# Chunk A loads of the next batch go ahead of waiting chunk C loads in the load list of a Fourier-mixing and SwiGLU kernel

## The chip, the cores and the metric

One NeuronCore of a Trainium2 chip. The time is the device time of one execution in microseconds (us), as the median of several runs. A traced execution gives the profile; its clock starts at the first instruction of the program.

## The reference

The input x has 8 batches of 3008 rows of 256 values. Each batch goes through a two-dimensional Fourier transform, of which the real part is kept; its rows then go through a gated feed-forward block.

```python
X = np.fft.fft(np.fft.fft(x, axis=1), axis=2).real   # x: (8, 3008, 256)
x = X.reshape(8 * 3008, 256)
g = x @ w_gate                                       # w_gate, w_val: (256, 1536)
out = (g / (1 + np.exp(-g)) * (x @ w_val)) @ w_out   # w_out: (1536, 256)
```

Inputs and output are float32; the matrix products inside the kernel run in bfloat16.

## The kernel before, in words

**Two kinds of work share the engines.** The transform uses the symmetries of a real input: rows that mirror each other are added and subtracted ("folded"), on POOL for all batches but the first, and the folded rows are multiplied by tables of sines and cosines on PE. What results are two tiles per 512 columns, Pt and Qt, from which the rows of the output at a frequency k and at M - k follow as a sum and a difference (the letters p and m, "plus" and "minus", in the names below). The feed-forward block works through 24 such tiles of columns, each in 12 units (one unit for each 128 of the 1536 hidden columns), 288 units in all. The program is written out unit by unit in this order, and each engine executes its own instructions strictly in the order in which they are written (a manual schedule).

**One unit.** PE makes the gate g and the value v from Pt and Qt (`part_a`, L737), adds the correction for the minus half one unit later (`part_b`, L774), and between these multiplies earlier hidden tiles by w_out (`OWork`, L697). ACT applies the gate function (L749, L764, L778, L782). The product of gate and value is taken by DVE (L765, L783), or, in six of twelve units of a tile from tile 3 on ("split" units), by POOL (L757 for hp, L779 for hm), with DVE preparing the plus and minus values first: es (L752) and two vv (L754, L756). The vv tiles have four buffers, so a third split unit's first vv waits for POOL's product of the first split unit. Accumulators lie in PSUM: three banks named g, three named v, two named o. The finished o is copied to an output buffer ev by ACT (L703, L706; four buffers, one for 256 rows), and written to memory by SP (L709, two or three DMAs for one buffer).

**The loads.** Each batch is loaded in two chunks: chunk A into XA (20 DMAs: 16 small at L129, 4 large at L131), chunk C into XC (39 DMAs at L140, L143, L145). XA holds one batch; XC has two halves, for two batches. All these loads and all output writes are issued by SP, in the order of the program. A load may be issued when the fold that read the old contents is past its last read (L165). Eight semaphores are used in turn for SP's DMAs, so that one DMA is issued only when the one eight before it has landed.

**The load list.** Loads are not written into the program at once, but put into a list, `loads`. At the head of each unit `run_loads` writes the first three of it (if the first is of chunk A) or the first six. When a fold has taken its last read of XA or XC, two units later `load_next` puts the next loads at the end of the list: after a chunk A fold those of A for the next batch; after a chunk C fold those of C for the next two batches (78 DMAs, marked with the number of the first of them). When a fold begins whose loads still wait, `fold_step` writes out all of the list up to the last of these loads ("rush").

**Folds on POOL.** A fold of one half of a chunk is seven steps: two with SDf (L165), which read XA or XC, and then EOf, Af, CE and BB (L168 to L184) from SDf. The steps are spread over the units (`spread`) and stand in POOL's order among the products L757 and L779. The fold of C(2) and C(3), batches 2 and 3, is spread over units 25 to 44, that of A(2) over 45 to 63, that of A(3) from 65 on.

**At the place of the change.** At unit 11 the 78 loads of C(2) and C(3) are put into the list; they follow the loads of A(1). At unit 22 the loads of A(2) are put at its end: 36 loads of C(3) are then still waiting. At units 23, 24 and 25 six loads each are written, and at unit 25 the fold of C(2) begins and rushes the last 18. A(2) follows at three a unit. Later batches' A loads are put into a list that is empty.

Of the kernel before, what the change touches and what calls it, by code (L numbers as in the profile page):

```python
# [31 lines left out]
def kernel(  # L32
# [8 lines left out]
    nc = tc.nc  # L41
# [76 lines left out]
    def up_block(b, j, n):  # L118
        return rows_at(b, 2 * j - 1, [[2 * D, n], [R * D, 4], [1, 2 * D]])

    def down_set(b, a, j, L, n):

        return rows_at(b, R * (a + 1) - 2 * j, [[2 * L * D, n], [-2 * D, L], [1, 2 * D]])
# [3 lines left out]
    def load_a(b, q):  # L127
        X3 = XA.rearrange("p a q d -> p a (q d)")
        return ([lambda h=h: q.dma_start(out=X3[LA * h:LA * (h + 1), 0:4, :],  # L129
                                         in_=up_block(b, JA - LA * h, LA)) for h in range(NA)] +  # L130
                [lambda a=a: q.dma_start(out=X3[:, 4 + a, :], in_=down_set(b, a, JA, LA, NA)) for a in range(4)])  # L131

    def load_c(b, q):
        bb = b % 2
        steps = []
        for qq in range(2):
            p0 = 64 * qq
            for h in range(NC_):
                up = rows_at(b, 2 * (JC - LC * h) - 1 + qq, [[2 * D, LC], [R * D, 4], [1, D]])
                steps.append(lambda p=p0 + LC * h, up=up: q.dma_start(out=XC[p:p + LC, 0:4, bb, :], in_=up))  # L140
            for a in range(4):
                down = rows_at(b, R * (a + 1) - 2 * JC + 1 - qq, [[2 * LC * D, NC_], [-2 * D, LC], [1, D]])
                steps.append(lambda p=p0, a=a, down=down: q.dma_start(out=XC[p:p + NCR, 4 + a, bb, :], in_=down))  # L143
        pm = 64 + NCR
        steps.append(lambda: q.dma_start(out=XC[pm:pm + 1, 0:4, bb], in_=rows_at(b, 0, [[R * D, 1], [R * D, 4], [1, D]])))  # L145
        return steps
# [681 lines left out]
    def load_next(what):  # L828
        kind, b = what
        if kind == "A":  # L830
            if b + 1 < B:
                loads.extend((("A", b + 1), fn) for fn in load_a(b + 1, nc.sync))
        else:
            b = b // 2 * 2 + 2
            if b < B:
                loads.extend((("C", b), fn) for fn in load_c(b, nc.sync) + load_c(b + 1, nc.sync))
# [34 lines left out]
    loads = []  # L871
# [3 lines left out]
    for i, u in enumerate(units):  # L875
# [25 lines left out]
        for what in act_at.pop(i, ()):  # L901
            load_next(what)
# [38 lines left out]
```

## Time and profile before

| | before |
|---|---|
| median of 3 runs | 690.73 us (689.88 to 691.08) |
| the profiled execution | 688.43 us |
| its span, first to last instruction | 686.7 us |
| PE busy | 662.1 us (96%) |
| POOL busy | 570.3 us (83%) |
| DVE busy | 513.5 us (75%) |
| ACT busy | 432.4 us (63%) |
| granted TensorE clock over the span | 0.995 |
| read from memory, written to it | 29.39 MB, 24.65 MB |

PE is the matrix engine, DVE the vector engine, ACT the scalar engine, POOL the general-purpose engine; SP only issues DMAs. The page's second part cuts the span into 40 slices of 17.2 us and gives the busy share of each engine in tenths; "PEclk" is the clock that the matrix engine was granted. The chain of work that ended last is followed back from the last instruction. A timeline row gives start, duration, engine, source line, operation, "written <- read" tiles, shapes and count; a bracket at its end gives how long the engine was idle before and what ended that. SPq is SP's issuing sequencer. Rows of windows give the stretch, its length, busy time and count of PE, PE's weight loads, DVE, ACT and POOL, then the granted clock, the busy share of the DMA engines and GB/s. Where the profile names a DMA as the releaser of a wait, the name can be that of a neighbour on the same semaphore.

### The profile page before, as it was taken

What the parts mean: (1) busy time and instruction counts of PE and PEld (TensorE: products, weight loads), DVE (VectorE), ACT (ScalarE), POOL (GpSimd) and SP (SyncE); (2) the same over time, 40 slices, a digit from 0 to 9 for tenths busy, and PEclk for the clock granted to TensorE, in tenths of its full rate; (3) what the DMA queues carried; (4) which work ended last, traced back from release to release, by engine and by line L of the source; (5) the groups of instructions that cost most, each with busy time, mean ns of one, the idle gap of its engine ahead of it and who ended that gap; (6) DMA issues with size and microseconds to landing.
All of it is one profiled execution on the core that took longest, in us unless ns stands there. A gap on an engine that the chain in (4) does not pass through costs nothing.

```text
span 686.7 us, 13388 instructions
## 1 busy us (share of the span) xinstructions
PE 662.1 (96%) x4374; PEld 414.7 (60%) x4374; DVE 513.5 (75%) x919; ACT 432.4 (63%) x764; POOL 570.3 (83%) x558
## 2 busy tenths in 40 slices
PE   7989999999799999999999999999999999999997
PEld 5446665665455666565665666656666666656676
DVE  8886668786567877777777787777777787788862
ACT  7676655665456666565666666666666666666663
POOL 9991977999499999999998998998999655668920
PEclk9999999999989999999999999999999999999999
DMA  9555225323512412235125111117111011111112
GB/s 229 105 87 109 74 59 156 110 67 107 165 31 66 121 47 68 72 95 160 36 62 145 38 44 35 48 40 155 36 48 48 32 41 38 46 32 47 47 47 70
DMA packets 49767, 52.56 MB, mean 77 GB/s; under 512 B 7130, under 2 KB 41026, under 8 KB 49698
## 3 DMA queue, kind: packets, MB, share of 16 engines
q1 hardware_dynamic: 46514, 49.35, 26.4%
q0 software_dynamic: 3184, 2.36, 2.4%
q8 instruction: 34, 0.56, 0.4%
q14 instruction: 35, 0.29, 0.1%
HBM read 29.39 MB, written 24.65 MB: 79 GB/s over the span
## 4 chain that ended last, share of the span: by engine, by line
PE 80%; DVE 8%; POOL 4%; issue 4%; ACT 1%; DMA 1%; SPq 0%; DVEq 0%; ACTq 0%; POOLq 0%
PE o L697 31%; PE v L737 16%; PE g L737 15%; PE g L774 8%; PE v L774 4%; PE v L572 3%; DVE vv L756 2%; DVE Pt L604 1%; PE g L572 1%; POOL hm L779 1%; DVE es L752 1%; DMA out_dram<-ev 1%; DVE vv L754 1%; POOL SDf L165 1%; PE g L880 1%
## 5 line engine op out<-in xcount | busy, mean ns | idle before, releaser
L757 POOL TENSOR_TENSOR hp<-sgv,vv 128x512 bf16<-128x512 f32 (+1 forms) x126 | 160.3, 1274 | 39.9 <-DVE vv L754 26.8
L697 PE MATMUL o<-Wo,hm 128*128 128x256 bf16 (+2 forms) x1140 | 170.5, 274 | 0.0
L697 PE MATMUL o<-Wo,hp 128*128 128x256 bf16 (+2 forms) x1140 | 169.6, 273 | 0.0
L779 POOL TENSOR_TENSOR hm<-sgv,vv 128x512 bf16<-128x512 f32 (+1 forms) x126 | 159.8, 1273 | 9.9 <-ACT sgv L778 8.2
L697 PEld LDWEIGHTS <-hp 128*128 128x128 bf16 (+2 forms) x1140 | 112.0, 98 | 68.2 <-issue 7.8
L697 PEld LDWEIGHTS <-hm 128*128 128x128 bf16 (+2 forms) x1140 | 112.4, 99 | 65.8 <-issue 6.4
L752 DVE SCALAR_TENSOR_TENSOR es<-bc,w,v 128x512 f32<-128x512 f32 (+1 forms) x126 | 93.7, 744 | 52.4 <-PE v L737 52.3
L765 DVE TENSOR_TENSOR hp<-sg,v 128x512 bf16<-128x512 f32 (+2 forms) x162 | 107.8, 665 | 33.0 <-ACT sg L764 32.1
L783 DVE TENSOR_TENSOR hm<-sg,v 128x512 bf16<-128x512 f32 (+2 forms) x162 | 107.4, 663 | 24.2 <-ACT sg L782 15.3
L782 ACT ACTIVATE sg<-g 128x512 f32<-128x512 f32 (+2 forms) x162 | 94.7, 585 | 46.8 <-PE g L774 46.0
L764 ACT ACTIVATE sg<-g 128x512 f32<-128x512 f32 (+2 forms) x162 | 94.5, 583 | 38.2 <-PE g L737 35.6
L737 PE MATMUL v<-Pt,Wp 128*128 128x512 bf16 (+2 forms) x288 | 108.4, 376 | 6.3 <-DVE vv L756 6.2
L737 PE MATMUL g<-Pt,Wp 128*128 128x512 bf16 (+2 forms) x288 | 108.5, 377 | 1.5 <-ACT sgv L778 1.1
L778 ACT ACTIVATE sgv<-g 128x512 f32<-128x512 f32 (+1 forms) x126 | 75.4, 598 | 53.7 <-PE g L774 39.8
L737 PE MATMUL g<-Qt,Wq 128*128 128x512 bf16 (+2 forms) x288 | 108.2, 376 | 0.5 <-DVE Qt L604 0.5
L774 PE MATMUL g<-Qt,Wm 128*128 128x512 bf16 (+2 forms) x288 | 108.1, 375 | 0.0
L754 DVE SCALAR_TENSOR_TENSOR vv<-v,es 128x512 f32<-128x512 f32 (+1 forms) x126 | 87.0, 690 | 18.6 <-POOL hp L757 1.0
L756 DVE SCALAR_TENSOR_TENSOR vv<-v,es 128x512 f32<-128x512 f32 (+1 forms) x126 | 85.7, 680 | 12.9 <-POOL hm L779 12.8
L749 ACT ACTIVATE sgv<-g 128x512 f32<-128x512 f32 (+1 forms) x126 | 75.1, 596 | 30.6 <-PE g L737 23.0
L165 POOL TENSOR_TENSOR SDf<-XA 128x1024 f32<-128x1024 f32 x28 | 66.0, 2363 | 24.8 <-DMA XC<-in_x_dram 14.7
L737 PEld LDWEIGHTS <-Wp 128*128 128x128 bf16 x576 | 56.4, 98 | 45.3 <-issue 7.7
L703 ACT COPY ev<-o 128x512 f32<-128x512 f32 x90 | 52.7, 586 | 34.3 <-PE o L697 29.1
(170 smaller groups left out, 731.0 us busy)
## 6 DMA issues: line engine op xcount, KB each, us to landing
out_dram<-ev SPq DMA_DIRECT2D x96, 128.0 KB
XA<-in_x_dram SPq DMA_DIRECT2D x32, 256.0 KB
XA<-in_x_dram SPq DMA_DIRECT2D x112, 64.0 KB
XC<-in_x_dram SPq DMA_DIRECT2D x210, 16.0 KB
XC<-in_x_dram SPq DMA_DIRECT2D x56, 60.0 KB
out_dram<-ev SPq DMA_DIRECT2D x12, 120.0 KB
out_dram<-ev SPq DMA_DIRECT2D x10, 112.0 KB
XA<-in_x_dram SPq DMA_DIRECT2D x1, 1024.0 KB
```

Of the source, the lines that this page charges most:

```text
L697: nc.tensor.matmul(ps[:n, j, :], hts[minus][:, f, c:c + n], Wo[:, f, :], start=(f == 0), stop=(f == nF - 1))
L737: nc.tensor.matmul(ps[:, :w], Wt[:, gv, fs], src[:, :w], start=start, stop=stop, skip_group_check=True)
L752: stt(es[:, :w], bc[t][:, :w], w0[:, f:f + 1], e[:, :w], op0=Alu.mult, op1=Alu.add)
L754: stt(vp[:, :w], o[:, :w], -0.5, es[:, :w], op0=Alu.mult, op1=Alu.add)
L756: stt(vm[:, w - 1::-1], o[:, :w], 0.5, es[:, :w], op0=Alu.mult, op1=Alu.add)
L757: nc.gpsimd.tensor_tensor(hts[t][0][:, f, :w], sg[:, :w], vp[:, :w], op=Alu.mult)
L764: nc.scalar.activation(sg[:, :w], g[:, :w], AF.Silu)
L765: nc.vector.tensor_tensor(hts[t][0][:, f, :w], sg[:, :w], v[:, :w], op=Alu.mult)
L774: nc.tensor.matmul(ps[:, :w], Wm[:, gv, f * P:(f + 1) * P], Qt[:, :w], start=False, stop=True, skip_group_check=True)
L779: nc.gpsimd.tensor_tensor(hts[t][1][:, f, :w], sg[:, :w], v[:, :w], op=Alu.mult)
L782: nc.scalar.activation(sg[:, :w], g[:, :w], AF.Silu)
L783: nc.vector.tensor_tensor(hts[t][1][:, f, w - 1::-1], sg[:, :w], v[:, :w], op=Alu.mult)
```

## The change

`load_next` puts the loads of the next batch's chunk A not at the end of the list but ahead of the first waiting chunk C load, where there is one.

```diff
@@ load_next @@
         kind, b = what
         if kind == "A":
             if b + 1 < B:
-                loads.extend((("A", b + 1), fn) for fn in load_a(b + 1, nc.sync))
+                at = next((k for k, (w_, _) in enumerate(loads) if w_[0] == "C"), len(loads))
+                loads[at:at] = [(("A", b + 1), fn) for fn in load_a(b + 1, nc.sync)]
         else:
             b = b // 2 * 2 + 2
             if b < B:
```

Written out, the program differs on SP alone, and in one stretch: after the third load of C(3) come the 20 loads of A(2), with one group of three outputs after the sixth, and then the other 36 loads of C(3). At units 23 to 25 three A loads each are written, and at unit 25 the fold of C(2) rushes 11 loads of A and, because all 78 loads carry the mark of C(2), 36 of C(3). The outputs that stood between the loads of A(2) now follow the last load of C(3). The orders of PE, DVE, ACT and POOL are unchanged.

```
before                                     after
C(3): 15 loads                             C(3): 3 loads
outputs x3                                 A(2): 6 loads
C(3): 24 loads                             outputs x3
A(2): 6 loads                              A(2): 14 loads
outputs x3                                 C(3): 36 loads
A(2): 9 loads                              outputs x12
outputs x3
A(2): 5 loads
outputs x6
C(4) ...                                   C(4) ...
```

## The prediction

> **What bounds the kernel now.** I read the page first (totals, the row of slices, the chain), then each engine's timeline where the change can act, then busy time by windows there.
>
> ```profile
> span 686.7 us, 13388 instructions
> PE 662.1 (96%) x4374; PEld 414.7 (60%) x4374; DVE 513.5 (75%) x919; ACT 432.4 (63%) x764; POOL 570.3 (83%) x558
> ...
> POOL 9991977999499999999998998998999655668920
> ...
> PE 80%; DVE 8%; POOL 4%; issue 4%; ACT 1%; DMA 1%; SPq 0%; DVEq 0%; ACTq 0%; POOLq 0%
> ```
>
> PE is busy 96% of the span and holds 80% of the chain, so a microsecond that PE loses is lost unless it would have been lost anyway. POOL is full through most slices too, except the sixth (86 to 103 us) and the eleventh (172 to 189 us). Those two dips decide this case. Of the six times that a batch queues the next chunk A, only one finds chunk C loads waiting, the one at unit 22: 36 loads of C(3) wait, and A(2) now goes ahead of them. So the change acts once, near 86 us. From the C(4) loads on, SP's list is the same as before.
>
> ```profile
> 77.04 4.67 POOL L165 TENSOR_TENSOR SDf<-XA 128x1024 f32<-128x1024 f32 x2
> ...
> 106.83 2.36 POOL L165 TENSOR_TENSOR SDf<-XC 128x1024 f32<-128x1024 f32 x1 [7.90 <-DMA XA<-in_x_dram]
> ...
> 112.63 1.22 POOL L779 TENSOR_TENSOR hm<-sgv,vv 128x480 bf16<-128x480 f32 x1
> ...
> 156.58 2.37 POOL L165 TENSOR_TENSOR SDf<-XA 128x1024 f32<-128x1024 f32 x1
> ...
> 174.66 1.27 POOL L757 TENSOR_TENSOR hp<-sgv,vv 128x512 bf16<-128x512 f32 x1
> 185.94 2.34 POOL L165 TENSOR_TENSOR SDf<-XA 128x1024 f32<-128x1024 f32 x1 [10.00 <-DMA out_dram<-ev]
> ...
> 229.60 1.27 POOL L757 TENSOR_TENSOR hp<-sgv,vv 128x512 bf16<-128x512 f32 x1 [0.39 <-DVE vv L754]
> ```
>
> In POOL's timeline (start, duration, instruction, idle before in brackets) POOL stands idle for 7.90 us until 106.83, where the fold of C(3) begins: its loads are the ones that SP has just issued (below). From there POOL runs without a gap to 175.93, then waits 10.00 us for A(3).
>
> **The loads, on SP.**
>
> ```profile
> 85.47 5.22 SPq L140 DMA_DIRECT2D XC<-in_x_dram  x15
> ...
> 104.80 0.64 SPq L145 DMA_DIRECT2D XC<-in_x_dram  x1
> 105.54 2.12 SPq L129 DMA_DIRECT2D XA<-in_x_dram  x6
> 107.76 1.15 SPq L709 DMA_DIRECT2D out_dram<-ev  x3
> 108.95 4.21 SPq L129 DMA_DIRECT2D XA<-in_x_dram  x9
> 113.27 1.27 SPq L709 DMA_DIRECT2D out_dram<-ev  x3
> 114.65 0.30 SPq L129 DMA_DIRECT2D XA<-in_x_dram  x1
> 115.17 2.53 SPq L131 DMA_DIRECT2D XA<-in_x_dram  x4
> 117.81 3.10 SPq L709 DMA_DIRECT2D out_dram<-ev  x6
> 121.01 3.11 SPq L140 DMA_DIRECT2D XC<-in_x_dram  x6
> ...
> 134.13 0.84 SPq L709 DMA_DIRECT2D out_dram<-ev  x2
> ...
> 168.04 2.02 SPq L129 DMA_DIRECT2D XA<-in_x_dram  x6
> ```
> ```profile
> SPq L140 <- DMA XA<-in_x_dram: 2.2, 2, 1.6
> ```
>
> SP issues back to back here, so order is time. A(2)'s 20 loads occupy 105.54 to 117.70, less the two groups of outputs between them: 12.16 - 1.24 - 1.49, about 9.4 us. After the change they follow the third C(3) load, at about 86.6. They need not wait there, since the fold of A(1) last reads XA at 81.71 (77.04 + 4.67). The other 36 C(3) loads come behind them.
>
> Three prices for the shift of C(3): at least 8.1 us, at the unhindered pace of the first row (5.22/15 for each of 16 loads, plus 2.53); 9.4 as A(2) was issued; at most 9.4 + 2.2 = 11.6, if C loads wait behind the four large A loads as they did for 2.2 us at the head of C(4) (the row of SP's waits). I take 11.0: this order, C behind large A, is the one that row shows. The last C(3) load goes from 104.80 to 115.8, and C(3)'s fold from 106.83 to 117.8.
>
> What A(2) gains is nothing: its fold already runs without a wait before it (POOL has no gap between 109 and 176). Four output groups (the rows at 107.76, 113.27 and 117.81) move from between the A loads to behind C(3), to about 116.5; the total work up to C(4) is equal, so C(4) still begins near 121.
>
> **What stands behind the late fold.** Behind it in POOL's order is the product hm (112.63 to 113.85), for which DVE waits already, and PE behind DVE.
>
> ```profile
> 113.88 0.66 DVE L756 SCALAR_TENSOR_TENSOR vv<-v,es 128x480 f32<-128x480 f32 x1 [0.71 <-POOL hm L779]
> ```
> ```profile
> 112.39 0.59 ACT L703 COPY ev<-o 128x512 f32<-128x512 f32 x1 [0.78 <-DMA XA<-in_x_dram]
> 112.87 0.58 ACT L778 ACTIVATE sgv<-g 128x480 f32<-128x480 f32 x1
> ...
> 120.52 0.59 ACT L703 COPY ev<-o 128x512 f32<-128x512 f32 x1 [0.27 <-PE o L697]
> ```
> ```profile
> 114.72 0.48 PE L572 MATMUL g<-Tab,BBa 128*128 128x376 bf16 x2
> ...
> 115.98 0.37 PE L737 MATMUL v<-Pt,Wp 128*128 128x480 bf16 x1
> ```
>
> The vv at 113.88 goes to 124.9; PE's v at 115.98 needs the bank that it frees, at 125.5: PE is 9.5 us late. A second lock lies inside the first: by the four output buffers, ACT's copy at 112.39 needs the output group of 107.76, now issued near 116.5 and landed near 120; the sgv behind it frees the bank for the matmuls at 114.72. So PE stands from about 115 to 121.5, does some 2 us, and stands again until 125.5. Both locks overlap; only the later counts.
>
> **The stop that goes away.** Later PE stands anyway:
>
> ```profile
> 183.66 0.38 PE L737 MATMUL g<-Qt,Wq 128*128 128x512 bf16 x1
> 190.27 0.59 PE L737 MATMUL v<-Pt,Wp 128*128 128x512 bf16 x1 [6.23 <-DVE vv L756]
> ```
> ```profile
> 160.00:170.00 10.00, 8.40 (x59) 5.32 (x58) 6.40 (x10) 5.01 (x10) 10.00 (x12) 1.00 0.40 113
> 184.00:189.00 5.00, 0.04 (x1) 0.00 (x0) 0.00 (x0) 0.00 (x0) 3.06 (x2) 0.99 0.27 89
> 189.00:190.00 1.00, 0.00 (x0) 0.00 (x0) 0.48 (x1) 0.48 (x1) 1.00 (x2) 0.50 0.00 0
> 190.00:195.00 5.00, 4.73 (x16) 2.24 (x16) 2.77 (x5) 1.79 (x4) 5.00 (x4) 0.50 0.00 0
> 195.00:196.00 1.00, 1.00 (x6) 0.43 (x5) 0.34 (x1) 0.60 (x1) 1.00 (x3) 0.63 0.00 0
> ```
>
> POOL waits for A(3), PE for POOL: 6.23 us, and then 5.8 us at the granted clock 0.50 (the last column but two), worth 2.9 us. In terms of full-clock work PE resumes at 190.27 + 2.9 = 193.2. Ten microseconds earlier PE lost 1.6 us (8.40 busy of 10), to an output that SP issued late. A kernel that reaches these places 11 us later meets loads that have arrived. That is the cover; the sum is what is left over it.
>
> SP does not follow PE's delay at first: it issues the output of the copy at 120.52 (done 121.11) only at 134.13. With the copy 9.5 to 12.4 us later 0.6 us of that slack remains, more in the next groups. It does follow POOL once: A(3) may overwrite XA when A(2)'s last fold read ends, 156.58 + 2.37 = 158.95, which becomes 169.9; SP stood at A(3)'s first load at 168.04, so A(3) comes 1.9 us later. Against that, two output groups of some 256 KB each ran beside A(3)'s last loads, and will come after them:
>
> ```profile
> 181.00:182.00 1.00, 1.00 (x8) 0.67 (x7) 0.69 (x1) 0.91 (x2) 0.00 (x0) 1.00 1.03 260
> ```
>
> At the 260 GB/s of that row (last column) their 0.5 MB took up to 1.9 us of the transfers' time, so A(3) lands between 0 and 1.9 us later than before.
>
> **The sum.** By POOL: the product at 174.66 ends at 175.93 + 11.0 = 186.9, A(3) lands between 185.9 and 187.8, so the fold at 185.94 begins 1.0 to 1.9 us later; the gap before 229.60 gives back 0.4, leaving +0.6 to +1.5. By PE: its delay of 9.5 us grows if the clock halves after the early stop. The stop is longer than the 6.23 us that halved it at 189; half clock from 125.5 for 5.8 us costs 2.9, a delay of 12.4. Then the g at 183.66, after which PE stood at 184.04, ends at 184.04 - 1.6 + 12.4 = 194.8, against 193.2 before: +1.6. Without the half clock PE keeps POOL's 11.0 and arrives at 193.4: +0.2. The later of both paths counts; I take +1.6. The profiled execution lasts 688.43 us (span 686.7 and 1.7 around it) and becomes 690.0; the median of the runs is 2.3 us above it, so I forecast 692.3.
>
> [...]
>
> **Rivals.** No change (0.36): the half clock is short or absent and A(3) lands early; the result is +0.6, 691.3. For it: the restart at 121.5 interrupts the early stop. Against it: even the shorter stop exceeds 6 us.
>
> Faster (0.10): the 20 loads cost only the 8.1 us of unhindered issue. Then POOL is free at 184.0, A(3) is not held back (158.95 + 8.1 is before 168.04) and lands up to 1.9 us earlier; PE arrives at 184.04 - 1.6 + 8.1 = 190.5 rather than 193.2, without half clock. The smaller gain decides: -1.9, so 688.8. It decides below a shift of 9.1 us, where A(3) is no longer held. Against it: A(2) took 9.4 where it stands.
>
> The delay is not absorbed (0.05): SP is held by a late copy at 134.13, where 0.6 us is left. A(3) then comes later by each microsecond more, up to the whole 11.0, and the time reaches 701.7. It needs 9 us more of PE delay than any row gives.
>
> My forecast, +1.6, has 0.49. The difference that a measurement here can tell from none is about 0.2%, 1.4 us. The range reaches from an even trade to a shift of 11.6 with an SP held 2 us: 690.0 to 694.5; its own part is 692.1 to 694.5. Faster 0.10, same 0.36, slower 0.54.
>
> **What would show it.** POOL's gap before the first C(3) fold grows from 7.90 to about 19, a PE stop with half clock appears at 115 to 131, and the gap of 10.00 before A(3)'s fold shrinks below 2 with PE's 6.23 us stop gone. The forecast is wrong if C(3)'s shift is under 9.1 us, if the late stop survives, or if the early half clock lasts much longer than 6 us.

## The result, and the profile after

The changed kernel takes 692.85 us in the median of 7 runs (691.52 to 695.0), the kernel before 690.73 (688.59 to 691.13, 7 runs). The ratio is 1.0037 with a 95% interval of 1.0022 to 1.0051: slower by 2.1 us. The profiled execution took 691.52 us (span 689.7) against 688.43 (686.7), so the two traces differ by 3.0 us of span, and the trace's differences are to be read against that.

The page of the changed kernel, its first lines and three rows of slices:

```profile
span 689.7 us, 13384 instructions
PE 662.2 (96%) x4374; PEld 414.9 (60%) x4374; DVE 513.4 (74%) x919; ACT 432.8 (63%) x764; POOL 570.3 (83%) x558
...
PE   8989996799999999999999999999999999999997
...
POOL 9991970999999999999999998998999755668920
PEclk9999999699999999999999999999999999999999
```

The same rows of PE and its clock on the page before:

```profile
PE   7989999999799999999999999999999999999997
...
PEclk9999999999989999999999999999999999999999
```

The work of each engine is as before. PE's dip has moved from the eleventh slice to the seventh and eighth, and the loss of granted clock from the twelfth to the eighth. POOL's dip in the eleventh slice is gone; the one in the sixth and seventh is deeper.

SP's timeline of the changed kernel, where the order differs:

```profile
86.78 2.00 SPq L129 DMA_DIRECT2D XA<-in_x_dram  x6
88.88 1.08 SPq L709 DMA_DIRECT2D out_dram<-ev  x3
90.22 4.98 SPq L129 DMA_DIRECT2D XA<-in_x_dram  x10
95.38 2.51 SPq L131 DMA_DIRECT2D XA<-in_x_dram  x4
97.94 6.58 SPq L140 DMA_DIRECT2D XC<-in_x_dram  x12
...
117.13 0.64 SPq L145 DMA_DIRECT2D XC<-in_x_dram  x1
117.87 5.63 SPq L709 DMA_DIRECT2D out_dram<-ev  x12
123.60 2.00 SPq L140 DMA_DIRECT2D XC<-in_x_dram  x6
...
171.72 2.02 SPq L129 DMA_DIRECT2D XA<-in_x_dram  x6
```

A(2) is issued 19 us earlier. The last load of C(3) goes from 104.80 to 117.13, 12.3 us later; the 12 C loads behind the A loads took 6.58 us, where 15 had taken 5.22. The first load of A(3) is issued at 171.72, where it was 168.04.

POOL's timeline of the changed kernel, the rows that answer to those shown before:

```profile
119.66 2.34 POOL L165 TENSOR_TENSOR SDf<-XC 128x1024 f32<-128x1024 f32 x1 [20.65 <-DMA out_dram<-ev]
...
169.34 2.35 POOL L165 TENSOR_TENSOR SDf<-XA 128x1024 f32<-128x1024 f32 x1
...
187.44 1.28 POOL L757 TENSOR_TENSOR hp<-sgv,vv 128x512 bf16<-128x512 f32 x1
188.66 2.37 POOL L165 TENSOR_TENSOR SDf<-XA 128x1024 f32<-128x1024 f32 x1
...
232.77 1.27 POOL L757 TENSOR_TENSOR hp<-sgv,vv 128x512 bf16<-128x512 f32 x1 [0.39 <-DVE vv L754]
```

C(3)'s fold begins 12.8 us later (106.83 to 119.66) after a wait of 20.65 us. The fold of A(3), 185.94 before, begins at 188.66 without any wait: of the 12.8 us 2.7 are left there. At the product of 229.60 the distance is 3.2 us, and it stays so to the end; 3.2 us is also what PE is late from 197 us of the kernel before on. Next the three engines that stand behind the late fold, each in its own timeline (PE, ACT, DVE):

```profile
123.80 0.79 PE L572 MATMUL g<-Tab,BBa 128*128 128x376 bf16 x2 [8.92 <-ACT sgv L778]
127.26 0.56 PE L737 MATMUL g<-Pt,Wp 128*128 128x480 bf16 x1 [1.94 <-ACT sgv L778]
128.02 0.60 PE L737 MATMUL v<-Pt,Wp 128*128 128x480 bf16 x1
...
196.07 0.38 PE L737 MATMUL v<-Pt,Wp 128*128 128x512 bf16 x1
```
```profile
120.52 0.58 ACT L703 COPY ev<-o 128x512 f32<-128x512 f32 x1 [8.93 <-DMA out_dram<-ev]
123.18 0.57 ACT L778 ACTIVATE sgv<-g 128x480 f32<-128x480 f32 x1 [2.07 <-POOL hp L757]
```
```profile
123.18 0.66 DVE L754 SCALAR_TENSOR_TENSOR vv<-v,es 128x480 f32<-128x480 f32 x1 [10.81 <-POOL hp L757]
126.64 0.66 DVE L756 SCALAR_TENSOR_TENSOR vv<-v,es 128x480 f32<-128x480 f32 x1 [2.81 <-POOL hm L779]
```

PE now stands 8.92 and 1.94 us here; its v of unit 41 goes from 115.98 to 128.02. The v that stood 6.23 us until 190.27 starts at 196.07 with no idle time before it. Windows of the changed kernel show the clock (last column but two):

```profile
117.00:118.00 1.00, 0.00 (x0) 0.00 (x0) 0.00 (x0) 0.00 (x0) 0.00 (x0) 1.00 0.25 74
118.00:119.00 1.00, 0.00 (x0) 0.00 (x0) 0.00 (x0) 0.00 (x0) 0.00 (x0) 0.50 0.38 102
119.00:123.00 4.00, 0.00 (x0) 0.00 (x0) 0.00 (x0) 0.58 (x1) 3.34 (x2) 0.50 0.58 178
123.00:127.00 4.00, 1.52 (x6) 0.34 (x6) 1.02 (x2) 1.39 (x3) 4.00 (x4) 0.50 0.42 129
127.00:132.00 5.00, 4.74 (x18) 2.38 (x17) 4.34 (x9) 1.72 (x4) 5.00 (x6) 0.53 0.25 64
132.00:133.00 1.00, 1.00 (x8) 0.32 (x7) 0.00 (x0) 0.25 (x1) 1.00 (x2) 1.00 0.37 92
```

Half clock (0.50) lasts from 118, some 3.1 us into the stop that begins at 114.88, to about 132, and half clock near 190 is gone.

### The profile page after: what moved, and what is told of

Its sections match the earlier page's. It is cut to its first block, busy times and chain, and to the rows that moved or that the text cites. A ratio compares the mean times of both kernels' runs of the same rounds, so it can differ in the third digit from the quotient of the medians.

```text
span 689.7 us, 13384 instructions
## 1 busy us (share of the span) xinstructions
PE 662.2 (96%) x4374; PEld 414.9 (60%) x4374; DVE 513.4 (74%) x919; ACT 432.8 (63%) x764; POOL 570.3 (83%) x558
## 4 chain that ended last, share of the span: by engine, by line
PE 76%; DMA 7%; DVE 6%; POOL 4%; issue 3%; SPq 3%; ACT 1%; POOLq 0%; ACTq 0%; DVEq 0%
PE o L697 30%; PE v L737 15%; PE g L737 15%; PE g L774 8%; DMA XA<-in_x_dram 3%; PE v L774 3%; DMA XC<-in_x_dram 3%; PE v L572 3%; DVE vv L756 2%; POOL SDf L165 1%; DVE Pt L604 1%; SPq L143 1%; PE g L572 1%; SPq L140 1%; DVE vv L754 1%
## 5 line engine op out<-in xcount | busy, mean ns | idle before, releaser
L754 DVE SCALAR_TENSOR_TENSOR vv<-v,es 128x512 f32<-128x512 f32 (+1 forms) x126 | 87.0, 690 | 29.3 <-POOL hp L757 11.8
```

The costliest lines, as they stand in the source:

```text
L754: stt(vp[:, :w], o[:, :w], -0.5, es[:, :w], op0=Alu.mult, op1=Alu.add)
```

## The experiments

**Is it the late stop that takes the delay back?** The theory: the change delays C(3), POOL and PE by some 13 us; the stop that the kernel before has at 184 to 196 us, because A(3)'s loads stand behind 78 loads of C(4) and C(5), takes about 10 of them back. So I removed this cover (the late stop), in the kernel before and in the changed one, by queueing C(4) and C(5) at unit 60, behind A(3).

```diff
-            act_at.setdefault(max(unit + 2, 11), []).append(what)
+            act_at.setdefault(60 if what == ("C", 2) else max(unit + 2, 11), []).append(what)
```

The kernel before with this line:

> The kernel before, with the 78 loads of C(4) and C(5) put into the list at unit 60 instead of unit 38, so behind the loads of A(3). Absorption theory: the late stop of the kernel before (POOL idle 10.00 us until 185.94, PE idle 6.23 us, then half clock) comes from A(3)'s loads standing behind those 78 on SP. It goes: A(3)'s first load follows A(2)'s last fold read (158.95 us), POOL's gap before A(3)'s fold is under 1 us, no half clock near 190, and the time falls by 7 to 11 us, to about 682. Rival (the late stop has another cause, for example the output buffers): the gap stays above 5 us and the time stays within 3 us of 690.7.

And the changed kernel with it:

> The changed kernel with the same late C(4) and C(5). Absorption theory: the change delays C(3)'s fold by about 13 us and only the late stop took 9 to 10 of them back; with no late stop left to take them back the change costs its whole delay, so this kernel is 10 to 13.5 us slower than the kernel before with late C(4), about 692 to 695, and little different from the changed kernel as it is. Rival (the change costs some 2 to 3 us by itself, for example by its half clock): about 2 to 3 us slower than the kernel before with late C(4), about 684.

Measured: 678.9 us for the kernel before with late C(4) (ratio to before 0.9836, 0.9819 to 0.9853), and 692.63 for the changed kernel with it (1.0033, 1.0021 to 1.0045). SP and POOL of the first:

```profile
118.33 35.14 SPq L709 DMA_DIRECT2D out_dram<-ev  x25
159.20 2.02 SPq L129 DMA_DIRECT2D XA<-in_x_dram  x6
```
```profile
107.08 2.36 POOL L165 TENSOR_TENSOR SDf<-XC 128x1024 f32<-128x1024 f32 x1 [7.77 <-DMA XA<-in_x_dram]
...
156.81 2.37 POOL L165 TENSOR_TENSOR SDf<-XA 128x1024 f32<-128x1024 f32 x1
...
177.20 2.36 POOL L165 TENSOR_TENSOR SDf<-XA 128x1024 f32<-128x1024 f32 x1 [1.02 <-DMA XC<-in_x_dram]
```

A(3)'s first load follows A(2)'s last read at once (159.18, 159.20), and the gap of 10.00 before A(3)'s fold is 1.02. POOL of the changed kernel with late C(4):

```profile
119.02 2.34 POOL L165 TENSOR_TENSOR SDf<-XC 128x1024 f32<-128x1024 f32 x1 [20.50 <-DMA out_dram<-ev]
...
189.02 2.37 POOL L165 TENSOR_TENSOR SDf<-XA 128x1024 f32<-128x1024 f32 x1 [0.70 <-DMA XC<-in_x_dram]
```

The delay of C(3)'s fold, 11.9 us here, is still 11.8 us at A(3)'s fold: nothing takes it back. Between these two kernels the change costs 13.7 us in the medians (12.2 in the profiled executions), against 2.1 between the kernels as they are. The rival of a cost of 2 to 3 us by itself falls. The changed kernel gains nothing from the late C(4) (692.85 and 692.63): its POOL reached A(3)'s fold without a wait already.

**Which lock holds PE?** A lock is here one of the two waits that the prediction named: POOL's late fold of C(3), and ACT's wait for an output buffer. The first kernel keeps the changed order but gives C(3)'s loads their own mark, so that they are written at six a unit and outputs stand between them again.

```diff
-                loads.extend((("C", b), fn) for fn in load_c(b, nc.sync) + load_c(b + 1, nc.sync))
+                loads.extend((("C", b + h), fn) for h in range(2) for fn in load_c(b + h, nc.sync))
...
-        if i == 0:
-            run_loads(max((k + 1 for k, (w_, _) in enumerate(loads) if w_ == what), default=0))
+        if j == 0:
+            due = (kind, b + q) if kind == "C" and b > 1 else what
+            run_loads(max((k + 1 for k, (w_, _) in enumerate(loads) if w_ == due), default=0))
```

> The changed kernel, but the loads of C(3) carry their own mark, so that the fold of C(2) does not rush them and they are written at six a unit up to unit 35; the outputs of the units between stand between them again, as in the kernel before. Theory that POOL's late C(3) fold is the lock that counts: ACT's copy no longer waits 8.9 us for an output buffer, but C(3)'s fold begins another 2 to 3.5 us later (three groups of outputs ahead of its end), near 122 to 123, PE still stands until the first vv is released, and the time is 2 to 4 us above the changed kernel's, about 695. Rival (the output buffers are the lock that counts): PE's early stop shrinks by several us and the time falls below 691.

Measured: 697.36 us (1.0094, 1.0076 to 1.0113), 4.5 above the changed kernel. ACT no longer waits for an output buffer. POOL and PE of this kernel:

```profile
125.81 2.34 POOL L165 TENSOR_TENSOR SDf<-XC 128x1024 f32<-128x1024 f32 x1 [25.01 <-DMA out_dram<-ev]
```
```profile
129.95 0.79 PE L572 MATMUL g<-Tab,BBa 128*128 128x376 bf16 x2 [13.33 <-ACT sgv L778]
```

C(3)'s fold is at 125.81, later than I had expected, and PE's first stop is 13.33 us. Some 1.8 us of that lateness are there before the change acts: in this trace, as in four others below, PE and POOL are already 1.5 to 1.8 us later than in the kernel before from about 17 us on, and delays read from such a trace must be taken less that. So POOL's late fold holds PE without any help of the output buffers. The four combinations of the two locks were then compared without the cover, so that each delay shows whole. "Folds swapped" puts, in the same units, the first half of A(2)'s fold ahead of C(3)'s, so that POOL follows the new order of the loads:

```diff
+    due2 = [s for s in seq if s[1] in (("C", 2), ("A", 2))]
+    at2 = sorted(s[0] for s in due2)
+    first = seq.index(due2[0])
+    order2 = [(w, i) for h in range(2) for w in (("C", 2), ("A", 2)) for i in range(7 * h, 7 * h + 7)]
+    assert seq[first:first + 28] == due2
+    seq[first:first + 28] = [(u, w, i) for u, (w, i) in zip(at2, order2)]
     fold_at = {}
```

Folds swapped (POOL's lock gone, outputs still behind C(3)):

> The changed kernel with late C(4) and C(5) loads (so with no late stop to take a delay back; median 692.6 as it was run), and with the folds in the order of the new loads: on POOL the first half of A(2) is folded in the units in which C(3) was, and C(3) after it. POOL then waits for nothing at unit 35; the output groups still stand behind all of C(3). Theory of two locks, each of which would hold PE alone: ACT's wait of some 8 to 10 us for an output buffer stays and with it a PE stop of 7 to 9 us and a half clock, so the time falls only to 688 to 691. Rival (POOL's late fold is the only lock that counts, as the prediction had it): it falls to 679 to 682.

Own marks for C(3) (output lock gone, POOL's lock left):

> The changed kernel with separate marks for C(3) (outputs stand between the loads again, so no output lock, but C(3)'s fold begins at about 125) and with late C(4) and C(5). Theory of two locks: POOL's late fold alone holds PE, for 17 to 19 us, with nothing to take it back: 695 to 698.5, as with separate marks alone (697.4). Rival (the output lock is needed for the loss): under 690.

Both (neither lock):

> The same, with POOL's folds in the order of the new loads as well: neither lock is left, A(2) is still loaded ahead of C(3). Theory of two locks: the early stop goes and the time is that of the kernel before with late C(4) and C(5), 678 to 681. Rival (loading A(2) first costs by itself, by the transfers or by SP): 5 us or more above that.

| with late C(4) and C(5) | POOL waits for C(3) | folds swapped |
|---|---|---|
| outputs behind C(3) | 692.63 us | 688.1 us |
| outputs between (own marks) | 697.1 us | 679.41 us |

Against 678.9 us without the change. With neither lock A(2) ahead of C(3) costs nothing that can be told (0.984 of before, 0.9809 to 0.9872; 0.9836 without the change). Either lock left alone costs many microseconds: 9.2 the output lock, 18.2 POOL's. But own marks do more than free the outputs: with outputs between the loads, C(3)'s fold begins at 127.36, 8.3 us later than the 119.02 with both locks. So 18.2 us is not the price of POOL's lock at the delay that the change gives it; that price was not measured alone. The output lock alone, ACT and PE with folds swapped:

```profile
120.94 0.59 ACT L703 COPY ev<-o 128x512 f32<-128x512 f32 x1 [7.77 <-DMA out_dram<-ev]
```
```profile
122.05 0.79 PE L572 MATMUL g<-Tab,BBa 128*128 128x376 bf16 x2 [5.60 <-ACT sgv L778]
```

PE's stop is 5.60 us, less than the 7 to 9 expected, while the time fell into the expected range. The half clock behind the stop (0.50 from 120 to 124 us) adds to it: PE is then 8.6 us later than in the kernel before with late C(4), 7.1 without the 1.5 us that were there before. Of the 9.2 us of the medians this trace so shows some 7.

**How does the cost grow with the loads put ahead?** With the cover in place, only the first 16 (the small ones) or 8 loads of A(2) go ahead; the others join the end of the list. The edit for 16 (for 8 the two numbers are 8):

```diff
-                loads[at:at] = [(("A", b + 1), fn) for fn in load_a(b + 1, nc.sync)]
+                new = [(("A", b + 1), fn) for fn in load_a(b + 1, nc.sync)]
+                loads[at:at] = new[:16]
+                loads.extend(new[16:])
```

> Only the 16 small loads of A(2) go ahead of the 36 waiting loads of C(3); the 4 large ones (L131) follow them. Theory that the large loads make the following C loads wait (12 C(3) loads took 6.58 us behind them, 15 took 5.22 before): C(3)'s fold begins 6.5 to 8.5 us later than in the kernel before, rather than 12.8, near 114; the early stop of PE is under 6 us. By the absorption theory a delay under 9 us is covered wholly and the late stop is traded away: the time is 688 to 690.5, not slower than before. Rival (any A load ahead of C(3) costs in proportion, with nothing absorbed below 9 us): half to two thirds of the measured cost stay, 692.

> Only the first 8 loads of A(2) go ahead of the 36 waiting loads of C(3). Absorption theory: C(3)'s fold begins 3 to 4.5 us later than in the kernel before; PE's early stop is 1.5 to 3.5 us, too short to halve the clock; the late stop stays but shrinks by as much (POOL's gap of 10.00 to about 6, PE's 6.23 to about 3) and is then too short to halve the clock. The delay costs nothing and the half clock of the late stop (2.9 us) is saved: the time is 687 to 689.5, faster than before. Rival (each A load ahead costs in proportion, the measured 2.1 us for 20): 691.3 to 691.6.

Sixteen: 689.41 us (0.9989, 0.9976 to 1.0003), as expected in time, not told apart from no change. In that trace everything is already 1.5 us later before the change acts; less these, C(3)'s fold at 116.33 is 8.0 us late. PE's stop was 7.37 us, where I had expected under 6.

Eight: 692.95 us (1.0023, 1.0008 to 1.0038), not the 687 to 689.5 expected. SP, POOL and ACT of that kernel:

```profile
90.95 1.19 SPq L129 DMA_DIRECT2D XA<-in_x_dram  x2
92.76 6.24 SPq L140 DMA_DIRECT2D XC<-in_x_dram  x12
...
112.03 0.64 SPq L145 DMA_DIRECT2D XC<-in_x_dram  x1
112.72 2.18 SPq L129 DMA_DIRECT2D XA<-in_x_dram  x6
115.00 1.15 SPq L709 DMA_DIRECT2D out_dram<-ev  x3
...
174.09 2.02 SPq L129 DMA_DIRECT2D XA<-in_x_dram  x6
```
```profile
114.05 2.34 POOL L165 TENSOR_TENSOR SDf<-XC 128x1024 f32<-128x1024 f32 x1 [15.09 <-DMA XA<-in_x_dram]
...
191.68 2.34 POOL L165 TENSOR_TENSOR SDf<-XA 128x1024 f32<-128x1024 f32 x1 [6.65 <-DMA out_dram<-ev]
```
```profile
121.24 0.58 ACT L703 COPY ev<-o 128x512 f32<-128x512 f32 x1 [9.53 <-DMA out_dram<-ev]
```

Three things went past the expectation. Eight loads delayed C(3)'s fold by 7.2 us rather than 3 to 4.5, in part since the C loads behind them took 6.24 us for 12 (4.2 at the pace before). The output group of 107.76 moved to 115.00, and ACT waited 9.53 us for it: the output lock decides here, with a stop of 7.36 us on PE. And SP came later to A(3) than in the changed kernel (174.09 against 171.72), so that the late stop stayed as well, 6.65 us on POOL. The cost is not in proportion to the loads put ahead: it is about the same for 8 and for 20, and none for 16. Whether a stop of 1.5 to 3.5 us is too short to halve the clock, as I had taken it, was not shown: the clock halved some 5 us into the late stop of the kernel before (0.99 over 184 to 189, 0.50 behind) and 3.1 us into the early stop of the changed one.

The same eight, without the cover:

> The same 8 loads ahead, in the kernel with late C(4) and C(5) loads (median 678.9), where no late stop is left to take the delay back. Absorption theory: the whole early delay of 2 to 4.5 us reaches the end, so 681 to 683.5: the same edit that gains in the kernel before loses here. Rival: no loss here either, 679.

Measured: 685.88 us, 7.0 above the 678.9 of the kernel before with late C(4), again more than the 2 to 4.5 expected. ACT and PE of this kernel:

```profile
120.61 0.58 ACT L703 COPY ev<-o 128x512 f32<-128x512 f32 x1 [7.28 <-DMA out_dram<-ev]
```
```profile
121.72 0.79 PE L572 MATMUL g<-Tab,BBa 128*128 128x376 bf16 x2 [5.10 <-ACT sgv L778]
```

The price is again that of the output lock. C(3)'s fold is 6.6 us later than in the kernel before with late C(4) (113.68 against 107.08), 5.2 without what was there before the change acts; PE, behind its stop and the half clock, is 7.1 us late, counted in the same way, and about 6 us of that reach the end of this trace. The second half of the expectation, that the edit gains with the cover, is refuted by the run above it.

**Is it the half clock?** The changed kernel with 40 matmuls more ahead of the transform in unit 40, in a bank that the transform overwrites, to fill the early stop.

```diff
             every = slice(0, P)
+            if (b, part, eos) == (1, 1, (0,)):
+                for _ in range(40):
+                    nc.tensor.matmul(ps[0][0], Wp[:, 0, 0:P], Wq[:, 0, 0:T], start=True, stop=True,
+                                     skip_group_check=True)
```

> The changed kernel with 40 matmuls of 128x512 more (0.216 us apart in the trace, 8.6 us) ahead of the transform in unit 40, into a bank that the transform then overwrites: PE works through its early stop of 8.92 us and does not lose its clock; the result is the same. Theory that POOL's late fold holds PE and the half clock adds only what lies beyond it: the half clock of 118.4 to 132.1 goes or shrinks, PE's delay falls from 13.4 to between 11.3 and 12.8, POOL's stays at 12.8, and the time falls by 0 to 1.2 us, to 691.6 to 692.9. Rival (the half clock is the larger part of the change's cost): the time falls by 2 us or more, to the time before or below.

Measured: 693.68 us (1.005, 1.0029 to 1.0072), where the changed kernel has 1.0037. Windows of this kernel:

```profile
115.00:120.00 5.00, 5.00 (x25) 2.25 (x23) 0.00 (x0) 0.00 (x0) 0.18 (x1) 1.00 0.28 77
120.00:125.00 5.00, 4.88 (x25) 2.07 (x24) 0.66 (x1) 1.56 (x3) 5.00 (x3) 1.00 0.44 132
125.00:130.00 5.00, 2.55 (x16) 1.55 (x16) 3.04 (x7) 2.08 (x4) 5.00 (x6) 1.00 0.44 130
```

The clock stays at 1.00 through the stop, and no time is won: the median is 0.8 us above the changed kernel's, with intervals that overlap. The two traces show where the gain goes. Behind the stop PE is 11.3 us later than in the kernel before (11.8, of which 0.5 are there before the change acts), against 13.6 in the changed kernel. But POOL is as late as there, and PE waits for it, 0.62 us for hp at 173.20 and 0.34 us for CEa at 181.38. At the unit that the kernel before reaches at 173 us PE is 12.0 us late with the extra matmuls and 12.2 without. So the early half clock is covered by the wait for POOL, and worth some 0.2 us in these traces.

## Why the prediction was right, and where it was off

The time lies in the range and on the slower side as forecast: +2.1 us measured in the medians (+3.1 in the profiled executions), +1.6 forecast. The mechanism that carries it, a delay of over 10 us that a later stop takes back, was right. That the number came so near is partly luck: the shift was taken 1.8 us too small, and the half clock, by which the sum went to +1.6 on PE's path, was worth almost nothing, so that two errors worked against each other. Step by step:

- **The shift of C(3)** was the term that was mis-sized: 11.0 us taken, 11.6 as the most; measured 12.8. The 12 C loads behind the A loads took 6.58 us, 2.4 more than the pace of the 15 before (5.22 x 12/15 = 4.2), and the fold began 1.9 us after the last issue rather than 1.4. C(4) began at 123.60, not near 121 as the prediction had it; by the outputs ahead of A(3) (165.17 against 164.27) most of that was made up, and it did not count.
- **No gain from the earlier A(2)**: right. With both locks away the earlier A(2) gives 679.41, and without the change the time is 678.9.
- **POOL without a gap from C(3)'s fold to A(3)'s**: right; the whole 12.8 us arrives at the product that ended at 175.93 and now ends at 188.7.
- **The late stop goes and covers most of the delay**: right, and shown by its removal: 13.7 us without that cover, 2.1 with it. A(3)'s loads came 3.7 us later rather than 1.9, because A(2)'s last read ends at 171.69; but they were in place when POOL came. POOL's 12.8 us less the gap of 10.00 leave 2.7 at A(3)'s fold. PE's path is the later of the two, as in the prediction, but by only 0.4: PE was 12.2 us late at 183.44 of the kernel before, ran through the place of the late stop (5.8 us late at the v of 190.27) and of its half clock, and kept 3.2. The 0.4 us that the prediction took off for the gap before 229.60 did not come off; the gap is still 0.39.
- **Two locks on PE, of which the later counts**: right for this kernel, as far as the traces show, but incomplete twice. There is a third wait in it: ACT's sgv at 123.18 waits for POOL's hp, so PE's first stop ends at 123.80 and not at 121.5; the second stop ends at 127.26, and the v forecast for 125.5 starts at 128.02. And the output lock, which the prediction let fall as lying inside the other, cost 9.2 us where it stood alone (688.1 against 678.9).
- **The half clock**: it came at the early stop, as forecast, and lasted to 132, where 125.5 and 5.8 us more give 131. PE's delay grew by it from 11.7 to 13.6 us (9.5 and 12.4 forecast). But the prediction let this growth reach the end, as 2.9 us, and there it does not show: without the half clock PE waits for POOL instead, and of a delay 2.3 us smaller 0.2 are left at 173 us. So the choice between +0.2 and +1.6 on PE's path was made by a term that did not count; the larger shift made up for it. PE worked only 1.52 of the 4 us from 123, at a granted clock of 0.50, and the clock returned near 132 (0.53 over 127 to 132, 1.00 over 132 to 133), some 4.5 us after the work had become dense at 127.26.
- **The rivals**: "no change" rested on a short or absent half clock; a short one was not shown for this kernel (0.50 from 118 to about 132 in its trace), and the kernel with 40 matmuls more has none, and its time is no lower. "Not absorbed" was wrong for this kernel; without the cover the whole delay does reach the end (692.63 against 678.9), though for another reason than the late SP that it named. "Faster" needed a shift of C(3) below 9.1 us: 16 loads ahead came to 8.0 us and to 0.9989, not told apart from no change. The late stop is gone in that trace (POOL waits 1.26 us for A(3)), as the rival has it, but a gain of 1.9 us is not there.

## What to carry to other kernels

Ask of every stall that a delay meets later whether it would have been there anyway: a tuned kernel can hide most of a 13 us mistake behind a 10 us one, and the measured 0.4% tells of neither. When the order of loads on one issuing queue changes, follow three things: who needs the loads that are pushed back, in which order the consumer takes them, and which output transfers on the same queue move with them. The better version came from the stall that the change had covered: queueing 78 loads behind those that are needed sooner gives 678.9 us, 1.6% less than before.

## What the runs showed that I had not expected

Twelve C loads of 16 KB took 6.58, 6.96 and 6.75 us to issue behind twenty A loads with the four large at the end (the changed kernel, the same with late C(4), and folds swapped), and 5.02 behind sixteen small ones, where fifteen took 5.22 before. Behind eight small ones they took 6.24 us in one kernel and 5.13 in the other, with the same order of loads up to there. So the price of the large loads shows each time, and that of the small ones differs from one execution to the next. SP's waits fit this: over the whole execution its L140 loads waited 2.6 us for A loads before and 4.5 in the changed kernel. With eight semaphores in turn (so for all 704 of SP's DMAs in the traces of the kernel before and of the changed one), what stands eight places ahead is the likely cause, but no run here takes it apart. The kernel with eight loads ahead changes between A and C twice, and its SP reached A(3) 6 us later than in the kernel before.
